# A decode step on one core: attention's softmax and PV by groups of eight heads inside the K/V loop, larger K/V blocks, and a shorter start and end

## The chip, the cores and the metric

One core of one Trainium2 chip runs the whole program. The metric is the device time of one execution in microseconds (us), lower is better. A profiled execution has besides its time a span, from the first to the last recorded instruction; times inside the profile count from the start of the span. "PE" is TensorE's matmuls, "PEld" its weight loads, "DVE" VectorE, "ACT" ScalarE, "POOL" GpSimd and "SPq" the sequencer of SyncE, which issues nearly all transfers here. "PV" is the product of the softmax's weights with V, "PSUM" the memory that TensorE's matmuls write here, and a "ring" is a buffer whose slots are filled in turn and given back when they have been read.

## The reference

One token (x has 1 x 640 elements) goes through attention over a cache and then through a gated feed-forward, all in bf16:

```python
# x (1,1,640); k_cache, v_cache (1,32,4096,128); wq (640,4096); wo (4096,640)
# w_gate, w_up (640,1728); w_down (1728,640)
def _A_ref(x, k_cache, v_cache, wq, wo):
    W = min(4096, max(256, Sk // 4))                 # the last 1024 cached positions
    q = (x @ wq).reshape(B, Sq, 32, 128).transpose(0, 2, 1, 3)
    k, v = k_cache[:, :, Sk - W:, :], v_cache[:, :, Sk - W:, :]
    scores = jnp.einsum("bhqd,bhkd->bhqk", q, k) * (128 ** -0.5)
    o = jnp.einsum("bhqk,bhkd->bhqd", softmax(scores), v)
    return o.transpose(0, 2, 1, 3).reshape(B, Sq, 4096) @ wo

h  = x + _A_ref(layernorm(x), k_cache, v_cache, wq, wo)
h2 = h + (gelu(layernorm(h) @ w_gate) * (layernorm(h) @ w_up)) @ w_down
```

Some 33.9 MB must come in for one token: wq, wo, 1024 positions of K and V for 32 heads, and the three feed-forward weights. There is little arithmetic per byte.

## The kernel before

Everything is loaded by the SP queue in the order wq, K and V by pairs of heads, wo, gate and up, down. K goes through a ring of 8 heads; V stays whole. A head of K arrives as 128 partitions with 8 keys each. TensorE turns its eight 128x128 blocks round (matmuls against an identity), VectorE (even heads) or ScalarE (odd heads) copies the result out of PSUM, and eight one-column matmuls give that head's 1024 scores. Each matmul loads a 128x128 weight first, so it is two instructions of TensorE (the page counts 1316 matmuls and 1316 weight loads).

```python
        def issue_kv(p):                       # p: a pair of heads, 512 KB of K and 512 KB of V
            waits = []
            if p >= KR:                        # KR = 4 pairs in the K ring
                waits.append(ev_tr[2 * (p - KR) + 1])
            s = p % KR
            ev_k[p] = pg.dma("sync", kring[:, 2 * s:2 * s + 2, :], A_k_cache[0, 2 * p:2 * p + 2, S0:SK, :]. ..., st_k, waits=waits)
            ev_v[p] = pg.dma("sync", vbuf[:, 2 * p:2 * p + 2, :], A_v_cache[0, 2 * p:2 * p + 2, S0:SK, :]. ..., st_v)
        ...
        for h in range(NH):                    # the K/V loop
            do_transposes(h)
            if h % 2 == 1:
                p = h // 2 + KR
                if p < NH // 2:
                    issue_kv(p)
            do_evac(h)
            if h - LAG >= 0:
                do_scores(h - LAG)
        for h in range(NH - LAG, NH):
            do_scores(h)
        ev_scdone = ev_sc[NH - 1]
        ...                                    # loads of wo, gate, up, down are issued here
        ev_sts = pg.ins("dve", lambda e: e.tensor_copy(STs[:], psA[:, ST0:ST0 + 256]), waits=[ev_scdone])
        ...                                    # maximum, exp and sums for all 32 heads at once
        for h in range(NH):
            for c in range(8):                 # PV: 256 one-column matmuls
                ... e.matmul(psB[:, col:col + 1], vbuf[:, h, c * DH:(c + 1) * DH], Eb[:, c * 32 + h:c * 32 + h + 1], ...)
        ...
        for g in range(NH // 4):               # output projection: 160 one-column matmuls
            ...
```

x comes in first, with one element per packet, and is the first transfer of the queue. The result leaves through five matmuls and two ScalarE copies:

```python
        xsrc = A_x[0, 0].rearrange("(c p) -> p c", p=128)
        ev_x = pg.dma("sync", xT_b[:], xsrc, st_x, noncontig="tiny x transpose load")
        for k in range(NKC):
            ev_wq.append(pg.dma("sync", wq_v[:, k, :], A_wq[k * 128:(k + 1) * 128, :], st_wq))
        ...
        for c in range(NKC):
            ... e.matmul(dst, outT_b[:, c:c + 1], identb[:, :], start=True, stop=True)
        pg.ins("act", lambda e: e.activation(orow[0:1, 0:256], psD[0:1, 256:512], ACTF.Copy), waits=[ev_fint])
        ev_fin = pg.ins("act", lambda e: e.activation(orow[0:1, 256:D], psE[0:1, 0:384], ACTF.Copy))
```

Of the kernel before, what the change touches and what calls it, by code (L numbers as in the profile page):

```python
# [107 lines left out]
def bass_sequential_preLN__sliding_block_cached__geglu_ffn__decode_kernel(  # L108
# [13 lines left out]
    D = 640  # L122
# [9 lines left out]
    KR = 4  # L132
# [5 lines left out]
    with ExitStack() as es:  # L138
        cnt = [0]

        def S(shape, dt, name=None):
            cnt[0] += 1
            return es.enter_context(nc.sbuf_tensor(name or f"sb{cnt[0]}", list(shape), dt))

        def P(shape, dt, name=None):
            cnt[0] += 1
            return es.enter_context(nc.psum_tensor(name or f"ps{cnt[0]}", list(shape), dt))
# [8 lines left out]
        xT_b = S([128, NKC], BF16, "xT_b")  # L156
        xT = S([128, NKC], FP32, "xT")
        stack1 = S([128, 2 * NKC], FP32, "stack1")
        tot1 = S([128, 2], FP32, "tot1")
        mean1 = S([128, 1], FP32, "mean1")  # L160
        msq1 = S([128, 1], FP32, "msq1")
        var1 = S([128, 1], FP32, "var1")
        lnv1 = S([128, 1], FP32, "lnv1")
        rstd1 = S([128, 1], FP32, "rstd1")
# [6 lines left out]
        kring = S([128, 2 * KR, 1024], BF16, "kring")  # L171
# [6 lines left out]
        STs = S([128, 256], FP32, "STs")  # L178
        m12 = S([128, 2], FP32, "m12")
        m2 = S([128, 1], FP32, "m2")  # L180
        mrow = S([1, NH], FP32, "mrow")
        Dd = S([128, 256], FP32, "Dd")
        Eb = S([128, 256], BF16, "Eb")
# [7 lines left out]
        tot2 = S([128, 2], FP32, "tot2")  # L191
        mean2 = S([128, 1], FP32, "mean2")
        msq2 = S([128, 1], FP32, "msq2")
        var2 = S([128, 1], FP32, "var2")
        lnv2 = S([128, 1], FP32, "lnv2")
        rstd2 = S([128, 1], FP32, "rstd2")
# [19 lines left out]
        orow = S([1, D], BF16, "orow")  # L216
# [7 lines left out]
        QP0, ST0, LN1S, LN2S, GP0 = 0, 160, 416, 426, 436  # L224
        OT0, T10 = 0, 256
        AT0, UP0, FP0, MR0, MX0, RR0 = 0, 160, 230, 300, 428, 460
# [4 lines left out]
        st_k = pg.stream("d_k", 8)  # L231
        st_v = pg.stream("d_v", 8)
        st_wo = pg.stream("d_wo", 8)
# [3 lines left out]
        st_out = pg.stream("d_out", 1)  # L237

# [32 lines left out]
        xsrc = A_x[0, 0].rearrange("(c p) -> p c", p=128)  # L271
        ev_x = pg.dma("sync", xT_b[:], xsrc, st_x, noncontig="tiny x transpose load")
        ev_wq = []
        for k in range(NKC):
            ev_wq.append(pg.dma("sync", wq_v[:, k, :], A_wq[k * 128:(k + 1) * 128, :], st_wq))

        ev = pg.ins("dve", lambda e: e.tensor_copy(xT[:], xT_b[:]), waits=[ev_x])
# [4 lines left out]
            lambda e: e.matmul(psA[:, LN1S:LN1S + 2 * NKC], onesf[:, :], stack1[:, :], start=True, stop=True),  # L282
            waits=[ev_const, ev_stack1],
        )

        def ln_chain(ps_cols, tot, mean, msq, var, lnv, rstd, src_f32, dst_b16, wait_ev):
            ev = pg.ins(
                "dve",
                lambda e: e.tensor_reduce(tot[:], ps_cols.rearrange("p (a b) -> p a b", a=2), axis=AX.X, op=ALU.add),
                waits=[wait_ev],  # L290
            )
            ev = pg.ins("dve", lambda e: e.tensor_scalar(mean[:], tot[:, 0:1], 1.0 / D, None, op0=ALU.mult), waits=[ev])
            ev = pg.ins("dve", lambda e: e.tensor_tensor(msq[:], mean[:], mean[:], ALU.mult), waits=[ev])
            ev_var = pg.ins(
                "dve",
                lambda e: e.scalar_tensor_tensor(var[:], tot[:, 1:2], 1.0 / D, msq[:], op0=ALU.mult, op1=ALU.subtract),  # L296
                waits=[ev],
            )
            ev = pg.ins("act", lambda e: e.activation(lnv[:], var[:], ACTF.Ln, bias=eps_t[:, 0:1], scale=1.0), waits=[ev_var, ev_const])  # L299
            ev_rstd = pg.ins("act", lambda e: e.activation(rstd[:], lnv[:], ACTF.Exp, scale=-0.5), waits=[ev])  # L300
            ev = pg.ins(
                "dve",
                lambda e: e.tensor_scalar(dst_b16, src_f32, mean[:, 0:1], rstd[:, 0:1], op0=ALU.subtract, op1=ALU.mult),  # L303
                waits=[ev_rstd],
            )
            return ev

        ev_xn = ln_chain(psA[:, LN1S:LN1S + 2 * NKC], tot1, mean1, msq1, var1, lnv1, rstd1, xT[:], xn_b[:], ev_ln1mm)

        pg.wait("pe", ev_xn)  # L310
        for k in range(NKC):
            pg.wait("pe", ev_wq[k])
            for h in range(NH):
                pg.ins(
                    "pe",
                    lambda e, k=k, h=h: e.matmul(  # L316
                        psA[:, QP0 + h * NKC + k:QP0 + h * NKC + k + 1],
                        wq_v[:, k, h * DH:(h + 1) * DH],
                        xn_b[:, k:k + 1],
                        start=True,  # L320
                        stop=True,
                    ),
                )
        ev_qdone = pg.cur("pe")
# [9 lines left out]
        ev_k = [None] * (NH // 2)  # L334
        ev_v = [None] * (NH // 2)
        ev_tr = [None] * NH
        ev_evac = [None] * NH
        ev_sc = [None] * NH

        def kslot(h):  # L340
            return (h // 2) % KR * 2 + (h % 2)

        def issue_kv(p):
            waits = []
            if p >= KR:
                waits.append(ev_tr[2 * (p - KR) + 1])
            s = p % KR
            ev_k[p] = pg.dma(
                "sync",
                kring[:, 2 * s:2 * s + 2, :],  # L350
                A_k_cache[0, 2 * p:2 * p + 2, S0:SK, :].rearrange("h (q c) d -> q h (c d)", q=128),
                st_k,
                waits=waits,
            )
            ev_v[p] = pg.dma(
                "sync",
                vbuf[:, 2 * p:2 * p + 2, :],
                A_v_cache[0, 2 * p:2 * p + 2, S0:SK, :].rearrange("h (q c) d -> q h (c d)", q=128),
                st_v,
            )  # L360

        def do_transposes(h):
            waits = [ev_k[h // 2], ev_const]
# [14 lines left out]
        def do_evac(h):  # L378
# [6 lines left out]
            if eng == "dve":  # L385
                ev_evac[h] = pg.ins("dve", lambda e, bank=bank, slot=slot: e.tensor_copy(KT_sb[:, slot, :], psKT[:, bank, :]), waits=waits)  # L386
# [7 lines left out]
        def do_scores(h):  # L394
            waits = [ev_evac[h], ev_qT]
            slot = h % 4
            for c in range(8):
                col = ST0 + c * 32 + h
                ev = pg.ins(
                    "pe",  # L400
                    lambda e, c=c, col=col, slot=slot, h=h: e.matmul(  # L401
                        psA[:, col:col + 1], KT_sb[:, slot, c * 128:(c + 1) * 128], QT_b[:, h:h + 1], start=True, stop=True
# [5 lines left out]
        LAG = 2  # L408
        for p in range(min(KR, NH // 2)):
            issue_kv(p)  # L410
        for h in range(NH):
            do_transposes(h)
            if h % 2 == 1:
                p = h // 2 + KR
                if p < NH // 2:
                    issue_kv(p)
            do_evac(h)
            if h - LAG >= 0:
                do_scores(h - LAG)
        for h in range(NH - LAG, NH):  # L420
            do_scores(h)
        ev_scdone = ev_sc[NH - 1]

        ev_wo = []
        for g in range(NH // 4):
# [3 lines left out]
                    wo_v[:, 4 * g:4 * g + 4, :],  # L429
                    A_wo[g * 512:(g + 1) * 512, :].rearrange("(i p) m -> p i m", p=128),  # L430
# [3 lines left out]
            )  # L434
        ev_wg = []
# [5 lines left out]
        for j in range(6):  # L441
# [11 lines left out]
        ev_sts = pg.ins("dve", lambda e: e.tensor_copy(STs[:], psA[:, ST0:ST0 + 256]), waits=[ev_scdone])  # L453
        pg.ins("pe", lambda e: e.transpose(psB[:, T10:T10 + 128], STs[:, 0:128], identf[:, :]), waits=[ev_sts])  # L454
        ev_t1 = pg.ins("pe", lambda e: e.transpose(psB[:, T10 + 128:T10 + 256], STs[:, 128:256], identf[:, :]))
        ev = pg.ins(
            "dve",
            lambda e: e.tensor_reduce(m12[:], psB[:, T10:T10 + 256].rearrange("p (a b) -> p a b", a=2), axis=AX.X, op=ALU.max),
            waits=[ev_t1],
        )  # L460
        ev_m2 = pg.ins("dve", lambda e: e.tensor_reduce(m2[:], m12[:], axis=AX.X, op=ALU.max), waits=[ev])
        ev_t2 = pg.ins(
            "pe",
            lambda e: e.matmul(psC[0:1, MR0:MR0 + 128], m2[:, 0:1], identf[:, :], start=True, stop=True),  # L464
            waits=[ev_m2],
        )
        ev_mrow = pg.ins(
            "dve",
            lambda e: e.tensor_reduce(
                mrow[:], psC[0:1, MR0:MR0 + 128].rearrange("p (c h) -> p h c", c=4), axis=AX.X, op=ALU.max  # L470
            ),
            waits=[ev_t2],
        )
        ev_maxrep = pg.ins(
            "pe",
            lambda e: e.matmul(psC[:, MX0:MX0 + NH], onesf[0:1, :], mrow[0:1, :], start=True, stop=True),  # L476
            waits=[ev_mrow],
        )
        maxrep_b = psC[:, MX0:MX0 + NH][:, None, :].to_broadcast([128, 8, NH])
        ev_D = pg.ins(  # L480
            "dve",
            lambda e: e.tensor_tensor(
# [187 lines left out]
```

## Time and profile before

| | before |
|---|---|
| time, median of the five runs at hand then | 105.54 us (105.31 to 105.87) |
| span of the profiled execution | 103.3 us |
| moved from memory | 33.90 MB, 328 GB/s over the span |
| TensorE busy | 66.7 us, 1316 matmuls |
| scores of the last head end | 63.8 us |
| down projection starts / ends | 97.25 / 99.81 us |
| last weights have landed | 93.0 us |

### The profile page before, as it was taken

To read this page: it belongs to the slowest core of one execution; us is meant where nothing else is said; L and a number is where in the kernel's file an instruction comes from. 1 tells how busy PE (TensorE), PEld (TensorE's weight loads), DVE (VectorE), ACT (ScalarE), POOL (GpSimd) and SP (SyncE) were. 2 spreads that over 40 slices of the span, in tenths; PEclk is the share of its full clock that TensorE was granted. 3 is DMA by queue.
4 is the path that set the end of the run, shared out by engine and by line. 5 is a ranking of instruction groups with operands and counts; after the bars stand their busy time and mean duration, and the time that the engine had idled before them with its cause. 6 is when DMAs were issued, how large, how long until landed. Compare 5 with 4: busy or idle time off the path is not lost.

```text
span 103.3 us, 2837 instructions
## 1 busy us (share of the span) xinstructions
PE 66.7 (65%) x1316; PEld 62.2 (60%) x1316; DVE 19.8 (19%) x56; ACT 20.2 (20%) x26; POOL 1.5 (1%) x15
## 2 busy tenths in 40 slices
PE   0234430868888888888888885569667592597360
PEld 0134330758887888888888884249666481596350
DVE  0230000222222222222222221340002004102410
ACT  5010000033333333333333333010000000100002
POOL 5000000000000000000000000000000000000000
DMA  0999999999999999999999999999999999930000
GB/s 0 282 412 434 419 438 374 387 387 387 387 384 385 388 386 384 389 384 389 383 385 388 382 369 359 363 363 363 374 412 400 399 397 367 355 125 0 6 0 0
DMA packets 17612, 34.07 MB, mean 330 GB/s; under 512 B 1665, under 2 KB 7490, under 8 KB 16962
## 3 DMA queue, kind: packets, MB, share of 16 engines
q1 hardware_dynamic: 17602, 33.91, 89.0%
q8 instruction: 10, 0.16, 0.7%
HBM read 33.90 MB, written 0.00 MB: 328 GB/s over the span
## 4 chain that ended last, share of the span: by engine, by line
DMA 37%; PE 33%; SPq 14%; DVE 6%; issue 5%; ACT 2%; ACTq 0%
DMA kring<-in_A_k_cache_dram 37%; SPq L79 13%; PE psKT L371 7%; PE psB L507 7%; PE psC L538 5%; PE psA L568 3%; PE psC L568 3%; PE psC L610 2%; PE psA L401 1%; ACT KT_sb L390 1%; PE psC L476 1%; PE psA L554 1%; PE psC L519 1%; PE psC L464 1%; PE psB L454 0%
## 5 line engine op out<-in xcount | busy, mean ns | idle before, releaser
L371 PE MATMUL psKT<-identb,kring 128*128 128x128 bf16 x256 | 32.6, 309 | 7.0 <-DMA kring<-in_A_k_cache_dram 7.0
L371 PEld LDWEIGHTS psKT<-identb,kring 128*128 128x128 bf16 x256 | 24.7, 140 | 8.4 <-DMA kring<-in_A_k_cache_dram 8.4
L390 ACT ACTIVATE KT_sb<-psKT 128x1024 bf16<-128x1024 bf16 x16 | 16.4, 1023 | 40.6 <-PE psA L401 25.5
L386 DVE COPY KT_sb<-psKT 128x1024 bf16<-128x1024 bf16 x16 | 11.1, 692 | 30.8 <-PE psA L401 30.2
L401 PEld LDWEIGHTS psA<-QT_b,KT_sb 128*128 128x128 bf16 x256 | 13.0, 115 | 0.8 <-ACT KT_sb L390 0.8
L401 PE MATMUL psA<-QT_b,KT_sb 128*128 128x1 bf16 x256 | 12.5, 171 | 0.7 <-ACT KT_sb L390 0.7
L316 PE MATMUL psA<-xn_b,wbig 128*128 128x1 bf16 x160 | 5.0, 166 | 9.2 <-DMA wbig<-in_A_wq_dram 9.2
L316 PEld LDWEIGHTS psA<-xn_b,wbig 128*128 128x128 bf16 x160 | 4.7, 104 | 9.6 <-DMA wbig<-in_A_wq_dram 7.5
L507 PE MATMUL psB<-Eb,vbuf 128*128 128x1 bf16 x256 | 7.6, 165 | 1.8 <-issue 1.8
L507 PEld LDWEIGHTS psB<-Eb,vbuf 128*128 128x128 bf16 x256 | 7.5, 104 | 2.1 <-issue 2.1
L538 PE MATMUL psC<-OT_b,wbig 128*128 128x1 bf16 x160 | 4.6, 165 | 2.0 <-issue 1.2
L538 PEld LDWEIGHTS psC<-OT_b,wbig 128*128 128x128 bf16 x160 | 4.4, 104 | 2.2 <-issue 1.3
L299 ACT ACTIVATE lnv<-var,eps_t 128x1 f32<-128x1 f32 x2 | 0.6, 295 | 23.3 <-DVE var L296 23.3
L568 PE MATMUL psA<-hn_b,wg_sb 128*128 128x1 bf16 x70 | 3.2, 170 | 1.7 <-DVE hn_b L303 1.7
L568 PEld LDWEIGHTS psA<-hn_b,wg_sb 128*128 128x128 bf16 x70 | 2.8, 107 | 2.0 <-DVE hn_b L303 1.8
L610 PE MATMUL psC<-act_b,wd_sb 128*128 128x1 bf16 (+1 forms) x70 | 2.1, 165 | 2.4 <-DVE act_b L600 2.4
L610 PEld LDWEIGHTS psC<-act_b,wd_sb 128*128 128x128 bf16 (+1 forms) x70 | 2.0, 104 | 2.5 <-DVE act_b L600 2.4
L282 PE MATMUL psA<-stack,onesf 128*128 128x10 f32 x2 | 0.6, 362 | 4.4 <-DVE stack L279 4.4
L568 PE MATMUL psC<-hn_b,wu_sb 128*128 128x1 bf16 x70 | 3.2, 170 | 0.0
L282 PEld LDWEIGHTS psA<-stack,onesf 128*128 128x128 f32 x2 | 0.5, 310 | 4.4 <-issue 4.4
L568 PEld LDWEIGHTS psC<-hn_b,wu_sb 128*128 128x128 bf16 x70 | 2.8, 107 | 0.1
L327 DVE TENSOR_REDUCE QT_f<-psA 128x32 f32<-128x160 f32 x1 | 0.3, 325 | 12.8 <-PE psA L316 12.8
(75 smaller groups left out, 21.4 us busy)
## 6 DMA issues: line engine op xcount, KB each, us to landing
kring<-in_A_k_cache_dram SPq DMA_DIRECT2D x16, 512.0 KB, 8.6
vbuf<-in_A_v_cache_dram SPq DMA_DIRECT2D x16, 512.0 KB, 9.6
wbig<-in_A_wq_dram SPq DMA_DIRECT2D x5, 1024.0 KB, 9.5
wbig<-in_A_wo_dram SPq DMA_DIRECT2D x8, 640.0 KB, 10.7
wg_sb<-in_B_w_gate_dram SPq DMA_DIRECT2D x5, 432.0 KB, 10.6
wu_sb<-in_B_w_up_dram SPq DMA_DIRECT2D x5, 432.0 KB, 11.2
wd_sb<-in_B_w_down_dram SPq DMA_DIRECT2D x6, 320.0 KB, 11.2
wd_sb<-in_B_w_down_dram SPq DMA_DIRECT2D x1, 160.0 KB, 8.2
```

What stands on the lines that cost most here:

```text
L79: e.dma_start(out_ap, in_ap, **kw).then_inc(sem, 16)
L282: lambda e: e.matmul(psA[:, LN1S:LN1S + 2 * NKC], onesf[:, :], stack1[:, :], start=True, stop=True),
L316: lambda e, k=k, h=h: e.matmul(psA[:, QP0 + h * NKC + k:QP0 + h * NKC + k + 1], wq_v[:, k, h * DH:(h + 1) * DH], xn_b[:, k:k + 1], start=True,
L371: lambda e, c=c, bank=bank, s=s: e.transpose(psKT[:, bank, c * 128:(c + 1) * 128], kring[:, s, c * DH:(c + 1) * DH], identb[:, :]),
L386: ev_evac[h] = pg.ins("dve", lambda e, bank=bank, slot=slot: e.tensor_copy(KT_sb[:, slot, :], psKT[:, bank, :]), waits=waits)
L390: lambda e, bank=bank, slot=slot: e.activation(KT_sb[:, slot, :], psKT[:, bank, :], ACTF.Copy),
L401: lambda e, c=c, col=col, slot=slot, h=h: e.matmul(psA[:, col:col + 1], KT_sb[:, slot, c * 128:(c + 1) * 128], QT_b[:, h:h + 1], start=Tru ...
L464: lambda e: e.matmul(psC[0:1, MR0:MR0 + 128], m2[:, 0:1], identf[:, :], start=True, stop=True),
L507: lambda e, h=h, c=c, col=col: e.matmul(psB[:, col:col + 1], vbuf[:, h, c * DH:(c + 1) * DH], Eb[:, c * 32 + h:c * 32 + h + 1], start=True ...
L538: lambda e, h=h, m=m, col=col: e.matmul(psC[:, col:col + 1], wo_v[:, h, m * 128:(m + 1) * 128], OT_b[:, h:h + 1], start=True, stop=True),
L568: lambda e, k=k, m=m, msz=msz, col=col, wsb=wsb, ps=ps: e.matmul(ps[0:msz, col:col + 1], wsb[:, k, m * 128:m * 128 + msz], hn_b[:, k:k + 1 ...
L610: lambda e, k=k, m=m, ksz=ksz, col=col: e.matmul(psC[:, col:col + 1], wd_sb[0:ksz, k, m * 128:(m + 1) * 128], act_b[0:ksz, k:k + 1], start ...
```

## The change

Its intent is to take softmax and PV of the first three groups of eight heads out of the serial tail and lay them beside the K/V transfers; 60 of the output projection's 160 matmuls fill waits in the softmax of the last group. K and V come by blocks of four heads (1 MB each), the K ring holds 12 heads, and a group's steps are put on an agenda, to be emitted during later iterations of the loop. Besides, wo comes in four transfers instead of eight, and there are 260 dummy matmuls between the Q projection's chunks, meant to bring TensorE's clock up, a one-step shorter layer norm and GELU, x as five rows on ScalarE's queue with a small transpose, and a last step of one matmul and one copy.

The diff, cut to its core (renamed tiles and PSUM columns are left out):

```diff
-    KR = 4
+    HB = 4
+    NB = NH // HB
+    KR = 3
+    GH = 8
+    NG = NH // GH
...
+        ev_x = pg.dma("act", x5[:, :], A_x[0, 0].rearrange("(c p) -> c p", p=128), st_x)
-        xsrc = A_x[0, 0].rearrange("(c p) -> p c", p=128)
-        ev_x = pg.dma("sync", xT_b[:], xsrc, st_x, noncontig="tiny x transpose load")
...
+            for d in range(80 if k == 3 else 45):
+                pg.ins(
+                    "pe",
+                    lambda e: e.matmul(psD[:, 511:512], identb[:, :], identb[:, 0:1], start=True, stop=True),
+                )
...
-                kring[:, 2 * s:2 * s + 2, :],
-                A_k_cache[0, 2 * p:2 * p + 2, S0:SK, :].rearrange("h (q c) d -> q h (c d)", q=128),
+                kring[:, HB * s:HB * s + HB, :],
+                A_k_cache[0, HB * b:HB * b + HB, S0:SK, :].rearrange("h (q c) d -> q h (c d)", q=128),
...
+        def schedule_group(g, it0):
+            at(it0, lambda: g_step_stscopy(g))
+            at(it0 + 1, lambda: g_step_t1(g))
+            at(it0 + 2, lambda: g_step_row(g))
+            at(it0 + 3, lambda: g_step_mx(g))
+            at(it0 + 4, lambda: g_step_sums(g))
+            at(it0 + 4, lambda: g_step_pv(g, 0, 4))
+            at(it0 + 5, lambda: g_step_pv(g, 1, 4))
+            at(it0 + 6, lambda: g_step_rrep(g))
+            at(it0 + 6, lambda: g_step_pv(g, 2, 4))
+            at(it0 + 7, lambda: g_step_pv(g, 3, 4))
+            at(it0 + 8, lambda: g_step_ot(g))
...
-        for h in range(NH - LAG, NH):
-            do_scores(h)
+        for hs in range(NH - LAG, NH):
+            do_scores(hs)
+            if hs % GH == GH - 1:
+                schedule_group(hs // GH, it)
+            run_agenda(it)
+            it += 1
+        at(it, lambda: at_part(0, 0, 2))       # output projection of heads 0 to 3, and so on
+        at(it + 1, lambda: at_part(0, 1, 2))
+        at(it + 2, lambda: at_part(1, 0, 2))
...
-        for c in range(NKC):                   # five matmuls and two ScalarE copies
-            ...
+            lambda e: e.matmul(psD[0:NKC, FIN0:FIN0 + 128], outT_b[:, 0:NKC], identb[:, :], start=True, stop=True),
+        ev_fin = pg.ins("dve", lambda e: e.tensor_copy(orow5[:, :], psD[0:NKC, FIN0:FIN0 + 128]), waits=[ev_fint])
```

## The prediction

> **What bounds the kernel now.** I read the page's 40 slices first, then the stretches, the chain of waits in order of time, and the DMA issues. Numbers are microseconds (us) of the profile's span, 103.3; the measured median, 105.54, is 2.24 more, and I add that at the end.
>
> The slices (tenths of busy time in 2.6 us each):
>
> ```profile
> PE   0234430868888888888888885569667592597360
> DMA  0999999999999999999999999999999999930000
> ```
>
> The transfers are full from 2.6 to 90 us; nothing but TensorE and small work fills the last five slices. The stretches say the same with rates (columns: stretch, length, busy us and count of PE, PEld, DVE, ACT, POOL; clock; DMA share; GB/s):
>
> ```profile
> 28.00:60.00 32.00, 27.20 (x383) 26.21 (x381) 8.30 (x12) 11.82 (x13) 0.00 (x0) 1.00 1.05 386
> 75.00:90.00 15.00, 8.86 (x266) 8.42 (x265) 2.20 (x10) 0.50 (x2) 0.00 (x0) 1.00 1.04 390
> 90.00:103.30 13.30, 7.70 (x193) 6.98 (x189) 2.17 (x13) 0.96 (x3) 0.00 (x0) 1.00 0.11 36
> ```
>
> In the K/V stage one pair of heads takes 2.72 us, which is 1.05 MB at 386 GB/s, and TensorE has a small rest before each pair (start, length, work, idle time before it):
>
> ```profile
> 24.99 1.03 PE L371 MATMUL psKT<-identb,kring 128*128 128x128 bf16 x8 [0.43 <-DMA kring<-in_A_k_cache_dram]
> 25.82 0.40 PE L401 MATMUL psA<-QT_b,KT_sb 128*128 128x1 bf16 x8
> 26.08 1.01 PE L371 MATMUL psKT<-identb,kring 128*128 128x128 bf16 x8
> 26.89 0.40 PE L401 MATMUL psA<-QT_b,KT_sb 128*128 128x1 bf16 x8
> 27.70 1.04 PE L371 MATMUL psKT<-identb,kring 128*128 128x128 bf16 x8 [0.41 <-DMA kring<-in_A_k_cache_dram]
> ```
>
> So that stage is bound by the transfers with 0.4 of 2.7 us to spare on TensorE. Afterwards the chain changes hands (start, length, what):
>
> ```profile
> 63.37 0.44 PE psA L401 x8
> 63.83 0.43 DVE STs L453
> ...
> 68.63 5.39 PE psB L507 x181
> 74.02 1.80 issue
> 75.82 2.14 PE psB L507 x75
> ...
> 79.25 1.52 PE psC L538 x51
> 80.77 1.24 issue
> 82.01 3.89 PE psC L538 x109
> ...
> 97.25 2.56 PE psC L610 x70
> 99.83 0.24 DVE ffn L617
> ```
>
> From 63.8 on, softmax, PV, output projection, second norm, gate/up, GELU and down projection run in series, 39.5 us, while the weights for them land behind their backs. The last weights come here (KB each, us from issue to landing):
>
> ```profile
> wd_sb<-in_B_w_down_dram SPq DMA_DIRECT2D x1, 80.0 KB, 7.9
> ```
>
> The timeline of the issuing queue puts that last issue at 85.06, so it lands at 93.0. The down projection starts at 97.25, 4.3 us later. **Hence the bound: transfers to 63, TensorE's serial tail afterwards, and only about 10.3 us of the end come after the last landing.**
>
> [...] eight transposes of 314 ns each end within 1.03 us, (1.03-0.314)/7 = 0.102 apart. The page's clock of 1.00 is no evidence; the spacing is. [...] a block of 32 one-column matmuls in 0.99 us is (0.99-0.165)/31 = 27 ns apart, but 109 of them take 3.89 in the chain, 36 ns each, so I price long runs at 34 to 36 and short ones at 27. [...] the two "issue" rests, 1.80 and 1.24 us, lie 128 matmuls (256 instructions with their weight loads) apart, and the packed DMA records have 16 KB instruction packets at 73.4 and 79.6, 1.1 us each, just before TensorE resumes. [...]
>
> **The change part by part.**
>
> *Softmax and PV by groups of 8 heads inside the K/V loop.* Per group TensorE had 8 x 1.07 = 8.6 us of transposes and scores. It gains 64 PV matmuls, 64 x 0.027 = 1.7, and a small chain (transpose, row, maximum, sums, reciprocal), of which the old one's matmuls took 0.23 to 0.65 each; smaller ones, about 1.4 together. Sum 11.7 against 10.8 of transfers for the group: TensorE becomes the slower of the two by 8%, but the first 10 heads carry no such work, and K is now buffered for 12 heads instead of 8. DVE and ACT have room (8.3 and 11.8 of 32 us).
>
> *Dummy matmuls.* 45, 45, 45, 80, 45 behind the five wq chunks: 260 more, each with an increment. Chunks land 2.5 us apart; 77 matmuls at 0.034 take 2.6, the 112 take 3.8. That alone moves the first transposes from 19.55 to about 21.2. They also eat instructions: [...] I get rests of 1.8 and 1.6 us and the first transposes near 24. I choose 24.
>
> *Loop end.* 10 heads x 1.07 from 24 gives 34.7; 22 more at 1.07 = 23.5, three groups' extra work 9.4, the last evacuation and scores 1.0: 68.6, against 63.8. The K reissues (after 4, 8, 12, 16, 20 heads) come some 4 us before the queue runs dry, so transfers should not pause.
>
> *Tail.* After 68.6 only group 3 is left: its chain about 3.6 (old 4.4, with narrower tiles), with 60 projection matmuls hidden inside; PV 64 x 0.034 = 2.2; then 100 projection matmuls, 3.4; reduction 0.3. Sum 9.5, plus about 1 for one instruction rest: 79.1 against 85.9 + 0.3. Norm: old 3.1 to the first gate matmul less one DVE step 0.2, so 82.0. Gate/up 5.9 (the last wu landed at 73.0 + 13.7 = 86.7 by its issue and its longest landing, 0.8 earlier now, and its matmuls run last, after 87): 87.9. GELU 2.5 less one step 0.2: 90.2. Down projection 2.6: 92.8.
>
> *Start and end.* x goes to ACT's queue in five rows, so wq is issued 0.5 earlier, and 640 two-byte packets vanish (about 5 us over 16 engines, 0.3): the last landing moves from 93.0 to 92.2. Then five last matmuls and the reduction can start at 92.7. One final matmul and one DVE copy instead of five matmuls and two ACT copies: the 3.5 us from the old reduction to the end lose about 0.9, leaving 2.6.
>
> Sum: the later of TensorE's 92.8 and the landing's 92.7, then 2.6: span 95.4, and with 2.24 **97.7 us, 7.4% less**. Both limits meet within their errors.
>
> **The rivals.** *A: the weights' landing alone is the end.* If the dummies cost less than I charge, or the loop is quicker, TensorE waits for the last panel: 92.7 + 2.6 + 2.2 = 97.5, no better. For it: transfers already run at 1.04 to 1.07 share and no byte is removed; against it: 24.
>
> *B: TensorE gets late.* Each us added to the start, loop or tail comes through once it passes the landing. Two or three more instruction rests of 1.5, which dense one-column runs invite, make 99.5 to 101. For it: the two rests of the old tail[...].
>
> *C: the K ring starves the queue.* If transposes of block b finish after the queue is drained, every us of gap moves the landing. It needs TensorE 4 us later than I think; result 99 to 102.
>
> *D: the dummies warm the clock.* Transposes below 107 ns would bring the loop back to the transfers' pace, and the result falls to A, 97.5, not lower. Against it: 256 PV matmuls in a row were followed by gate/up no faster.
>
> **Range and chances.** A and D are a floor near 97.5, less if the stream starts and flows a little better (96.7). B and C stretch upwards, so the range is lopsided: 96.7 to 100.5. To miss 2% (103.4) both B and C would have to hit hard: faster 0.95, same 0.04, slower 0.01.
>
> **What would show it.** Right: last wd landing at 92 to 93 with DMA still full to 90; transposes starting near 24, 106 ns apart; no idle before them "<-DMA kring" after the first heads; scores ending near 68.6; gate/up starting near 82; down projection either running straight or waiting for wd. Wrong: gaps in the DMA slices (C); many "issue" rests of over 1 us (B); transposes 60 to 80 ns apart (D); the first transposes at 20 to 21 (my instruction count for the dummies fails, TensorE early, but the end unchanged); a last landing far from 92.2, which would move the result by the same amount.

The sum came to 92.8 us for TensorE and 92.7 for the landing, to 92.8 + 2.6 = 95.4 of span, and with 2.24 to 97.7. The rests of 1.8 and 1.6 us among the dummies, which put the first transposes near 24 instead of 21.2, were the author's estimate; without them TensorE would end near 90.0 and the landing alone, 92.7 + 2.6 + 2.24, gives 97.5. The 0.5 us by which wq is issued earlier is the time that SPq takes to issue the x load in the trace of the kernel before, 0.46 us.

The same trace has these numbers: most transposes start 106 or 107 ns after the one before (194 of 255 steps); the 640 two-byte packets of x took 5.02 us, all added up; in PV and in gate/up alike the median step between one-column matmuls is 27 ns, which is the "no faster" under rival D. The page's clock of 1.00 is no evidence because that trace holds no clock record at all.

## More of the kernel before

The page of the kernel before gives the busy time by engine, and among the transfer queues one for instructions (packets, MB, share of the 16 transfer engines' time):

```profile
PE 66.7 (65%) x1316; PEld 62.2 (60%) x1316; DVE 19.8 (19%) x56; ACT 20.2 (20%) x26; POOL 1.5 (1%) x15
...
q8 instruction: 10, 0.16, 0.7%
```

No compute engine is busy over two thirds of the time, and the 16 transfer engines, which the page has at 89.0%, stand idle in the last four slices, so no total tells what bounds the kernel; it has to be read stage by stage. The ten instruction packets of 16 KB each look like nothing at 0.7% of the transfer engines' time.

## The result, and the profile after

Ratios here are the mean time of one kernel's fast runs over that of the other's of the same rounds, so they are not quite the ratio of the medians quoted beside them.

| | before | after |
|---|---|---|
| median of all runs | 105.49 us (105.23 to 105.87, 15 runs) | 97.58 us (97.21 to 97.7, 8 runs) |
| ratio, 95% interval | | 0.9252 (0.9238 to 0.9266) |
| profiled execution: time / span | 105.59 / 103.3 us | 97.7 / 95.9 us |
| scores of the last head end | 63.8 us | 67.6 us |
| gate/up starts | 89.0 us | 81.5 us |
| down projection starts | 97.25 us | 89.67 us |
| last weights have landed | 93.0 us | 92.8 us |

The slices of the page after, and its instruction queue. Each digit is a 40th of the span, 2.4 us:

```profile
PE   0269828639997909999999999999699822994551
...
PEclk9999999999999999555555555555555555555555
DMA  2999999999999999999999999999999999999500
...
q8 instruction: 12, 0.20, 0.8%
```

TensorE is now full where it used to be at 8 tenths, and the slices without transfers at the end are two instead of four. The clock row is to be read with care: it has 9 for the first 38 us, but the packed clock record begins only at 28.05 us, and the 24 transposes at 22.80 below take 2.72 us, (2.72 - 0.31) / 23 = 0.105 apart, the same pace as later under the row's 5 (mostly 106 or 107 ns from 38.29 on). The K/V stage after (columns as in the prediction):

```profile
20.00:61.00 41.00, 37.21 (x670) 35.89 (x669) 14.24 (x36) 14.78 (x16) 0.00 (x0) 0.72 1.05 385
```

The transfers run at the same 385 GB/s in the K/V stage as before (386). So the change has not made the stream faster; it has filled TensorE beside it, and what is left between the last landing and the end of the span has gone from 10.3 us to 3.1.

TensorE's timeline after shows where it stood still (start, length, work, idle time before it and what ended that):

```profile
14.65 0.46 PE L341 MATMUL psD<-identb 128*128 128x1 bf16 x12 [2.12 <-issue]
...
20.84 0.89 PE L330 MATMUL psA<-xn_b,wbig 128*128 128x1 bf16 x28 [2.57 <-issue]
...
22.80 2.72 PE L404 MATMUL psKT<-identb,kring 128*128 128x128 bf16 x24
...
36.00 0.62 PE L404 MATMUL psKT<-identb,kring 128*128 128x128 bf16 x8 [2.23 <-DMA kring<-in_A_k_cache_dram]
...
38.37 1.01 PE L404 MATMUL psKT<-identb,kring 128*128 128x128 bf16 x8
...
78.10 0.40 PE L648 MATMUL psA<-OT_b,wbig 128*128 128x1 bf16 x9 [1.21 <-issue]
...
91.50 0.43 PE L758 MATMUL psC<-act_b,wd_sb 128*128 128x1 bf16 x10 [0.60 <-DMA wd_sb<-in_B_w_down_dram]
92.25 0.90 PE L758 MATMUL psC<-act_b,wd_sb 128*128 128x1 bf16 x20 [0.32 <-DMA wd_sb<-in_B_w_down_dram]
```

Three things are to be seen. Two rests of "issue" lie at the start, one among the dummies and one within the Q projection (before 20.84), and a third in the output projection: TensorE waits for nothing that the profile shows. Each time a 16 KB instruction packet has just gone through (it began at 12.07, 18.34 and 75.60, and TensorE resumed 2.50 to 2.58 us later), so I read them as waits for instructions. At 36.00 a head takes 0.62 us and TensorE had waited 2.23 us for K, while at 38.37 a head takes 1.01. And the down projection, which is last, twice waits for its own weights. The chain of waits says that this is what sets the end:

```profile
83.17 9.03 DMA wd_sb<-in_B_w_down_dram
...
92.25 0.95 PE psC L758 x20
...
93.71 0.28 PE psD L772
...
94.01 0.28 DVE orow L775
```

Before, no transfer was in the chain after 60.2 us. Now the last transfers of weights are in it, and from the end of the last matmul (93.20) to the end of the span it is 2.7 us, where before it was 3.5.

### The profile page after: what moved, and what is told of

Read it like the earlier page. It is cut to its first block, busy times and chain, and to the rows that moved or that the text cites. A ratio compares the mean times of both kernels' runs of the same rounds, so it can differ in the third digit from the quotient of the medians.

```text
span 95.9 us, 3397 instructions
## 1 busy us (share of the span) xinstructions
PE 72.5 (76%) x1596; PEld 68.7 (72%) x1596; DVE 23.2 (24%) x80; ACT 20.0 (21%) x27; POOL 1.5 (2%) x15
## 4 chain that ended last, share of the span: by engine, by line
SPq 37%; DMA 28%; PE 25%; issue 6%; DVE 1%
SPq L79 37%; PE psKT L404 10%; DMA kring<-in_A_k_cache_dram 10%; DMA wd_sb<-in_B_w_down_dram 9%; DMA wbig<-in_A_wq_dram 9%; PE psD L341 5%; PE psA L330 3%; PE psE L551 2%; PE psB L440 1%; PE psC L758 1%; PE psA L440 1%; PE psC L567 1%; PE psC L498 0%; PE psD L772 0%; DVE orow L775 0%
## 5 line engine op out<-in xcount | busy, mean ns | idle before, releaser
L341 PE MATMUL psD<-identb 128*128 128x1 bf16 x260 | 7.8, 165 | 2.1 <-issue 2.1
L341 PEld LDWEIGHTS psD<-identb 128*128 128x128 bf16 x260 | 7.4, 104 | 2.2 <-issue 2.2
L551 PE MATMUL psE<-Eb,vbuf 128*128 128x1 bf16 x256 | 8.9, 165 | 0.0
L551 PEld LDWEIGHTS psE<-Eb,vbuf 128*128 128x128 bf16 x256 | 7.9, 104 | 0.3
L648 PE MATMUL psA<-OT_b,wbig 128*128 128x1 bf16 x160 | 5.2, 166 | 1.6 <-issue 1.2
L648 PEld LDWEIGHTS psA<-OT_b,wbig 128*128 128x128 bf16 x160 | 4.9, 105 | 2.1 <-issue 1.5
L440 PE MATMUL psA<-QT_b,KT_sb 128*128 128x1 bf16 x128 | 6.1, 169 | 0.0
L440 PEld LDWEIGHTS psA<-QT_b,KT_sb 128*128 128x128 bf16 x128 | 6.1, 110 | 0.0
L440 PE MATMUL psB<-QT_b,KT_sb 128*128 128x1 bf16 x128 | 6.1, 168 | 0.0
L440 PEld LDWEIGHTS psB<-QT_b,KT_sb 128*128 128x128 bf16 x128 | 6.0, 109 | 0.0
```

Source lines behind the costliest of these rows:

```text
L341: lambda e: e.matmul(psD[:, 511:512], identb[:, :], identb[:, 0:1], start=True, stop=True),
L440: lambda e, c=c, col=col, slot=slot, h=h, ps=ps: e.matmul(ps[:, col:col + 1], KT_sb[:, slot, c * 128:(c + 1) * 128], QT_b[:, h:h + 1], sta ...
L551: lambda e, h=h, c=c, col=col: e.matmul(psE[:, col:col + 1], vbuf[:, h, c * DH:(c + 1) * DH], Eb[:, h * 8 + c:h * 8 + c + 1], start=True, ...
L648: lambda e, h=h, m=m, col=col: e.matmul(psA[:, col:col + 1], wo_v[:, h, m * 128:(m + 1) * 128], OT_b[:, h:h + 1], start=True, stop=True),
```

## The experiments

All ran on the same inputs; "before" in the same rounds had medians between 105.45 and 105.57 us. Times are medians with the lowest and highest run, ratios are to the kernel before. Unless said otherwise a kernel is the changed one with one edit (e5, e6, e10 and e12 have no dummies besides), and its output agreed with the reference. That agreement is weak evidence for attention here: with these inputs attention's part of the output is so small that three kernels which are wrong (e6, e9, e10) passed as well.

### e1: without the dummy matmuls

```diff
-            for d in range(80 if k == 3 else 45):
+            for d in range(0):
```

> The changed kernel without its 260 dummy matmuls. Theory A (the landing of the last weights is the end, and each 16 KB instruction packet holds up one of the 16 transfer engines by 1.1 us): two packets fewer, the slowest engine trails the first by 2 us at the last weights as in the kernel before, instead of 3.5, the last landing moves from 92.8 to about 91.5 and the time to 96.3. The clock never warms (transposes 107 ns apart all through), first transposes near 19.6 instead of 22.8. Rival B (the end does not depend on the instruction packets): last landing 92.6 to 92.8, time 97.3 to 97.6. Rival C (the warm clock from the dummies is worth something): slower than the changed kernel, 98.3 or more.

Measured: 97.50 us (97.36 to 97.6), 0.9238 (0.9223 to 0.9254). The transposes started at 19.74 instead of 22.80, the scores ended 1.2 us sooner (66.42), and the end did not move. Its chain has the same last link:

```profile
82.30 9.77 DMA wd_sb<-in_B_w_down_dram
```

Theory A's number, 96.3, was missed: nine packets were left before the last landing, not eight, and its spread stayed at 3.36 us (below). So 260 dummies neither help nor harm: the 3 us that they cost at the start are taken up by waits for K and for weights later. The clock rose without them too: the trace's clock record has full speed from 23.0 to 26.4 and from 60.6 to 67.4.

### e2: the kernel before with the new x load and the new end only

```diff
 (to the kernel before)
+        ev_x = pg.dma("act", x5[:, :], A_x[0, 0].rearrange("(c p) -> c p", p=128), st_x)
-        ev_x = pg.dma("sync", xT_b[:], xsrc, st_x, ...)
+        (one matmul, one VectorE copy and five rows out instead of five, two and one)
```

> The kernel before with only the new x load and the new final transpose and copy; softmax, PV and projection stay after the loop. Theory A (most of the gain comes from moving softmax, PV and projection into the loop): end shorter by 0.9, start sooner by 0.5 to 1.2, so 103.4 to 104.1, and 5.8 or more are left for the grouping. Rival (the start and end are the bulk): 101 or less.

Measured: 103.26 us (103.14 to 103.4), 0.9785 (0.9769 to 0.9802). Start and end are worth (1 - 0.9785) x 105.57 = 2.3 us of the 7.9. The other 5.6 belong to the rest: groups, blocks and ring, dummies, and the shorter norm and GELU.

### e3: the changed kernel with the old end

> The changed kernel with the old end: five matmuls into one row, two ACT copies. It lies behind the last landing, so theory A has it in full: 0.9 slower, 98.5. Rival (the output transfer with five rows costs as much as it saves): within 0.3 of the changed kernel.

The edit is the last hunk of the diff taken back. Measured: 98.47 us (98.31 to 98.5), 0.9332 (0.9316 to 0.9347), so 0.9 us more. Its chain of waits after the reduction:

```profile
93.45 0.37 PE psD L778 x2
93.82 0.33 PE psE L778 x3
...
94.17 0.37 ACT orow L781
```

These links and 0.37 us more of ScalarE's sequencer stand where the changed kernel has 0.28 and 0.28 us.

### e4: the changed kernel with the old x load

```diff
-        ev_x = pg.dma("act", x5[:, :], A_x[0, 0].rearrange("(c p) -> c p", p=128), st_x)
+        xsrc = A_x[0, 0].rearrange("(c p) -> p c", p=128)
+        ev_x = pg.dma("sync", xT_b[:], xsrc, st_x, noncontig="tiny x transpose load")
```

> The changed kernel with the old x load: 640 two-byte packets on the weights' queue before wq. The first wq chunk landed 1.27 us sooner in the changed kernel, K blocks too. Theory A (the stream is full, so what it starts later it ends later): last landing 1.2 later, 98.8. Rival (the last landing is set by the slowest transfer engine, which moved only 0.2 between the two kernels, not by the start): 0.0 to 0.4 slower.

Measured: 99.26 us (98.98 to 99.63), 0.9408 (0.9375 to 0.9441), 1.7 us more; the last landing was 94.0, 1.2 us later. The 640 two-byte packets ahead of wq (5.02 us of packet time in the trace before) cost more than I had estimated (0.8 with the issue).

### e5: down's weights with fewer, longer rows

```diff
-            for d in range(80 if k == 3 else 45):
+            for d in range(0):
...
-                B_w_down[j * 256:(j + 1) * 256, :].rearrange("(i p) m -> p i m", p=128),
+        wd_rows = B_w_down[0:1664, :].rearrange("(p j) m -> p j m", j=KC_FF - 1)   # four transfers
...
-    wsb[:, k, m * 128:m * 128 + msz]
+    wsb[:, k, m:m + 128 * (KC_FF - 1):KC_FF - 1] if m < KC_FF - 1 else wsb[:, k, F - msz:F]
```

> The changed kernel without dummies, and with the FFN's hidden units dealt to partitions as f = 13 p + m, so that w_down's rows come in packets of 3840 to 5120 bytes instead of 1280 (gate/up take every 13th column as weights). Theory A (the landing of the last weights is the end): 2.1 MB at about 395 instead of 342 GB/s, the rates of the 3456 and 1280 byte packets in the trace of before, is 0.8 us less, so 96.7. Rival (packets are not the limit, or the strided weight loads slow gate/up): 97.5[...].

Cut from the rival is a figure for slow weight loads, which no trace had shown. The two rates are those of the trace before: its 3456 byte packets took 139.8 ns on average and its 1280 byte ones 59.9, which over 16 engines is 396 and 342 GB/s.

Measured: 99.03 us (98.51 to 100.45; the slowest is the profiled one), 0.937 (0.9328 to 0.9412); the fast runs are 98.51 to 99.35. This kernel has no dummies, so it is to be held against e1 (97.50). In the only trace, of the slow run, the last landing came at 92.1, against 92.7 in e1. But for gate and up the weight columns now lie 13 apart, and this is slower on TensorE. A block of 14 of them in the timeline of e5:

```profile
80.94 1.08 PE L711 MATMUL psB<-hn_b,wg_sb 128*128 128x1 bf16 x14 [1.54 <-DVE hn_b L304]
```

The next block starts at 81.95, 1.01 us later, where the changed kernel's blocks follow each other in 0.58 (82.10 after 81.52). In the same trace the down projection's 70 matmuls, whose columns lie side by side, take 2.11 us, 0.028 apart, and these are 0.07 apart. Ten blocks made the down projection start at 93.4 instead of 89.7, and TensorE set the end. The sooner landing could not be cashed in; the version fails.

### What the packed records show of the last landing

The page counts 16 transfer engines, and the trace records 16 increments of a semaphore for each of these transfers, one by one. I read each increment as one engine that has ended its part; the trace does not name the engine. So it can be seen which transfer has a straggler. In the kernel before, the first and last increment of a transfer lie 0.7 us apart up to 13.6 us. Then an instruction packet (16 KB, 1.0 to 1.1 us long) goes through at 15.6 us, and from there one increment is over 1.3 us behind the first. After each further packet (28.7, 39.5, 50.4, 61.3, 73.4, 79.6, 85.7) the number of such late ones goes up by one, until there are eight, with the spread still at 2.0 to 2.1. In the changed kernel the packets come sooner, since it has more instructions, and with the ninth at 69.3 the spread jumps from 1.92 to 3.23: one increment is now over 2.6 us late, and later up to four. The transfers behind it stay that way to the end. The same jump, by 1.2 to 1.5 us, comes with the ninth packet wherever the stream has no gap: in e1 at 82.4 (2.05 to 3.52), in e3 at 69.6, in e4 at 68.5, in e5 at 82.5 and in e6 at 87.7 (1.89 to 3.07). This suggests that the packets go round eight engines, and the ninth delays one that is already late. The same reading of the last weights' transfer in every kernel that ran:

```text
kernel                    instruction packets   first      last       spread
                          begun before it       increment  increment
before                     8                    90.85      92.97      2.12
e2 (start and end only)    8                    90.04      91.92      1.88
e11 (below)                8                    89.83      91.93      2.10
e9 (below)                 8                    89.51      91.26      1.75
e12 (below)                8                    89.43      91.38      1.94
e1 (no dummies)            9                    89.32      92.68      3.36
e6 (below)                 9                    89.58      92.39      2.82
e5 (slow run)              9                    88.98      92.08      3.10
after                     11                    89.23      92.79      3.56
e3 (old end)              11                    89.28      92.52      3.24
e4 (old x)                12                    90.50      94.02      3.53
e7 (below)                13                    92.26      95.33      3.07
e8 (below)                12                    95.89      98.21      2.32
e10 (below)               11                   124.67     127.03      2.35
```

The time of the kernel waits for the last increment. In the changed kernel the first one came 1.6 us sooner than before, and the last only 0.2. (e8 and e10 are the exceptions with their smaller spreads. Their streams have gaps, and after one the late increments are gone: none is late at 49.8 us in e8 and at 97.1 in e10. In e7 the pause at 31 to 34 us takes the late ones from four to none but the one of a new packet, and the jump, from 1.83 to 3.35, comes only with the packet at 91.8, the thirteenth in all and the ninth since the pause. So in these runs what counts is the packets since the last gap.)

### e6: fewer TensorE instructions

```diff
-            for h in range(NH):
+            for h in range(NH if k == NKC - 1 else 0):      # Q: 32 matmuls instead of 160, no dummies
-                        psA[:, QP0 + h * NKC + k:QP0 + h * NKC + k + 1],
+                        psA[:, QP0 + h * NKC:QP0 + h * NKC + NKC],
```

> Wrong result on purpose: the changed kernel without dummies and with 32 Q matmuls instead of 160, all wq chunks still awaited, so that TensorE's stream is one 16 KB block shorter and nothing else moves. In the traces each instruction packet adds one late transfer engine, and the ninth makes one late twice: the trailing engine's delay goes from 2.0 to 3.5 us. Theory A (that ninth packet sets the last landing): the ninth packet comes after 88, the trail stays at 2.0, the last landing near 91.3 instead of 92.7, the time 96.0. Rival (the trail comes from elsewhere, such as the smaller packets of the last weights): 97.3 to 97.6.

Measured: 97.52 us (97.28 to 97.78), 0.9244 (0.922 to 0.9268). There were still nine packets, the ninth at 87.7 us, just ahead of the last transfers, and the last landing was at 92.39. So it did not test the theory as meant: a kernel with eight was needed.

### e9: eight instruction packets

```diff
 (to e6)
-                for c in range(8):
+                for c in range(0, 8, 2):                    # PV: 128 matmuls instead of 256
-                            psE[:, col:col + 1],
+                            psE[:, col:col + 2],
```

> Wrong result on purpose: as the run with fewer Q matmuls, and each PV matmul takes two columns of weights for two output columns, so 128 matmuls fewer again: in the run before this one the ninth instruction packet still came at 87.7, now there should be at most eight before the last landing. Theory A (the ninth packet sets the last landing): the trailing engine stays at 1.9 us to the end, the last landing near 91.4 instead of 92.4, time 96.4 to 96.6. Rival (the trail or the landing comes from elsewhere): 97.3 to 97.6.

Measured: 96.13 us (96.08 to 96.28), 0.9117 (0.9103 to 0.9131). The page counts eight instruction packets, and the landing that its chain waits for is 1.2 us sooner than after (82.23 + 8.81 against 83.17 + 9.03):

```profile
q8 instruction: 8, 0.13, 0.6%
```

```profile
82.23 8.81 DMA wd_sb<-in_B_w_down_dram
```

The spread of the last transfer is 1.75 us. The same bytes are moved, and the first increment is even 0.28 us later than in the changed kernel; only the stragglers are gone. Against e6 the difference is one packet, and 128 matmuls that lie on neither chain after 47 us.

### e7: 128 dummies more

```diff
-            for d in range(80 if k == 3 else 45):
+            for d in range(108 if k == 3 else 70):
```

> The changed kernel with 128 dummies more, one 16 KB block. First transposes 5 to 6 us later, near 28.5; the 2.9 us that TensorE waited for K at 30 and 34 are used up, so the scores end 3 us later, near 70.6, and the down projection, which needed no longer than 92.2 by TensorE alone, ends near 95.2, past the last landing. Theory A (two limits that nearly meet): 99.0 to 100.5. Rival (transfers hide TensorE by a wide margin): within 0.5 of 97.6.

Measured: 100.45 us (99.61 to 101.76; one run slow), 0.9494 (0.9446 to 0.9543); the fast runs are 99.61 to 100.66. The size is about as expected, the way is not the one of TensorE's tail. The rates by slice of its page, each 2.46 us:

```profile
GB/s 47 403 416 426 423 413 392 386 389 389 382 386 247 88 404 392 389 387 386 386 385 388 389 378 382 365 362 361 363 359 379 409 409 417 403 381 360 232 12 1
```

The stream pauses around 31 to 34 us (247 and 88 GB/s). The transposes started at 28.58, so the first ring slots were given back late: the next K block was issued at 32.40, 1.3 us after the last transfer in flight had begun to end (31.09). The pause goes into every later landing; the first increment of the last transfer is 3.0 us later than after. This is the prediction's rival C. It shows as well how much slack the changed kernel has: in it the same block is issued at 26.61, 4.7 us before the last transfer ahead of it begins to end (31.35).

### e8: a K ring of 8 heads

```diff
-    KR = 3
+    KR = 2
```

> The changed kernel with K buffered for 8 heads instead of 12. Block 2 of K can only be asked for when block 0 is transposed, at 26.6, and by then the queue holds nothing: V1 lands from 25.9 on. Theory A (the larger ring pays for the late start of TensorE): a gap of 2 to 2.5 us in the transfers, seen as a step in the landings after 26 us and kept to the end, 99.6 to 100.2. Rival (8 heads are enough as in the kernel before): within 0.4 of 97.6.

Measured: 100.85 us (100.31 to 103.12; the profiled run was slow), 0.9542 (0.949 to 0.9594); the fast runs are 100.31 to 101.33. The transfers paused between 20 and 45 us, where they moved 339 GB/s against 385 (from the slow run). With dummies ahead and blocks of four heads, 8 heads of K are too few.

### e11: start, end and blocks, but no groups

```diff
 (to e2)
-    KR = 4
+    HB = 4
+    KR = 3          # K and V by 1 MB blocks, ring of 12 heads; softmax and PV stay after the loop
```

> The kernel before with the new x load and the new end, and now also K and V in 1 MB blocks of four heads with a ring of 12 heads, but softmax, PV and projection still after the loop. Theory A (the blocks and the ring are worth nothing by themselves, only moving the work into the loop is): 103.0 to 103.5 as with the small transfers. Rival (larger transfers quicken the stream): 102 or less.

Measured: 103.84 us (103.2 to 104.08), 0.9836 (0.9802 to 0.987), against 103.26 for e2. Larger blocks and a longer ring bring nothing by themselves. So of the 7.9 us, 2.3 are start and end, and the rest comes with the groups, for which the ring gives the slack (e8). The one-step shorter norm and GELU were not tried alone; they are within that rest.

### e10: K and V with packets of 4 KB

```diff
-            for d in range(80 if k == 3 else 45):
+            for d in range(0):
...
-                A_k_cache[0, HB * b:HB * b + HB, S0:SK, :].rearrange("h (q c) d -> q h (c d)", q=128),
+                src[0, HB * b + x:HB * b + HB:2, S0:SK, :].rearrange("h (q c) d -> q h (c d)", q=64),   # x = 0, 1
```

> Wrong result on purpose, to price the transfers: the changed kernel without dummies, K and V in packets of 4 KB (two heads on 64 partitions each, two transfers per block, the same bytes) instead of 2 KB; all else works on the wrongly laid out data. Theory A (the landing is the end and the packet's size sets the rate: 3456 byte packets moved 6% more per time than 2048 byte ones): K and V take 40.9 instead of 43.4, last landing 90.3, then TensorE's own limit near 91.4 takes over, time 96.0. Rival (half of the partitions per transfer loses what the packets gain): 97.5 or slower.

Measured: 131.83 us (131.21 to 132.45), 1.2496 (1.2441 to 1.255). Each transfer now fills 64 partitions with packets twice as long. The stretch of the K/V stage in it:

```profile
20.00:85.00 65.00, 37.02 (x564) 35.77 (x565) 12.94 (x31) 13.81 (x15) 0.00 (x0) 1.00 1.04 216
```

At the same share of busy transfer engines (1.04) only 216 GB/s were moved instead of 385. The theory that led to it has fallen: whatever longer packets may give (in the trace before, 3456 byte packets moved 396 GB/s over 16 engines and 2048 byte ones, 88.0 ns each, 372), the arrangement as a whole costs far more. Packet size and half the partitions were not separated.

### e12: VectorE takes the scores of 12 heads

If eight packets are worth 1.3 us, a correct kernel should get there too. Here VectorE computes the scores of heads 1, 3 and 5 of each group (12 of 32) from K as it lies, a multiplication with q repeated over the partitions and a sum (0.61 and 1.22 us for a head in its chain of waits, 1.83 together). That saves TensorE 16 matmuls for each of them, and the dummies are gone too.

```diff
-            for d in range(80 if k == 3 else 45):
+            for d in range(0):
...
+        def do_offload(h):
+                lambda e, j=j, s=s, b=b: e.tensor_tensor(
+                    kq[:, b, :]. ..., kring[:, s, :]. ..., qrow[:, j, :][:, None, :].to_broadcast([128, 8, DH]), ALU.mult),
+                lambda e, b=b, col=col: e.tensor_reduce(
+                    STs[:, col:col + 8], kq[:, b, :].rearrange("p (c d) -> p c d", d=DH), axis=AX.X, op=ALU.add),
...
         for h in range(NH):
-            do_transposes(h)
+            if h % GH in OFF:              # OFF = (1, 3, 5)
+                do_offload(h)
+            else:
+                do_transposes(h)
```

> A version with right results that has TensorE's stream shorter: the changed kernel without dummies, in which VectorE computes the scores of 12 of the 32 heads (K times the head's q, spread over the partitions by three matmuls, then a sum over 128), so that 192 transposes and score matmuls, 378 instructions with their loads and less the three new ones, are gone from TensorE. Theory A (the last landing is the end, and the ninth instruction packet sets it): at most eight instruction packets before the last landing, trail 1.7 to 2.0 us, last landing 91.3, time 96.1 to 96.4. Rival (VectorE, about 1.8 us per head here, holds up the K ring or TensorE): a gap in the transfers or a softmax chain that waits for VectorE, 97.5 or more.

Measured, five runs: 96.25 us (96.06 to 96.39), 0.9125 (0.9101 to 0.9149). It beats both kernels. Its page and its chain:

```profile
PE 56.9 (60%) x1146; PEld 51.9 (55%) x1147; DVE 38.1 (40%) x95; ACT 21.6 (23%) x30; POOL 1.6 (2%) x16
...
q8 instruction: 9, 0.15, 0.7%
```

```profile
83.82 7.56 DMA wd_sb<-in_B_w_down_dram
```

The ninth packet comes at 90.7, after the last transfer has begun to land, so eight count. The last landing is 91.38 and its spread 1.94, as the table has it. TensorE has 450 matmuls fewer than in the changed kernel, 15.6 us of busy time, and the gain over it is 1.3 us, what the sooner landing gives: the end still hangs on the stream. Because the comparison on the chip hardly sees attention, this kernel was also compared with the reference in a simulation with weights and caches scaled up. Repeated with wq, wo and the caches 20 times as large, it gave relative errors under 0.01 for this kernel and for the changed one, and over 1 for e9, which is wrong.

## Why the prediction was right

The time was 97.58 us against 97.7 predicted, and the direction, the main mechanism and the size were right. By its steps:

- *The tail's work fits beside the stream.* Right. e11 shows that blocks and ring alone bring nothing, so the groups bring what start and end (2.3 us, e2) do not. The scores were predicted to end at 68.6 and did at 67.6; gate/up at 82.0, measured 81.5; down at 90.2, measured 89.67.
- *Dummies and instruction rests.* The rests at the start were 2.12 and 2.57 us instead of 1.8 and 1.6, the first transposes at 22.80 instead of 24. e1 shows that all of this leaves the end where it is.
- *A third rest.* Of the rests that rival B feared in the tail there was one, 1.21 us, as the sum had allowed (about 1).
- *K waits.* That the transposes would have no idle time for K before them after the first heads was wrong: there were waits of 0.68 and 2.23 us. TensorE was ahead of the stream, since it began 1.2 us sooner than predicted and by the next point; no run separates the two.
- *Clock.* The prediction counted on transposes 106 ns apart throughout. Rival D was half right: from 28.05 to 38.29 the clock record has full speed, and the transposes in it are 55 to 56 ns apart, with scores among them, but TensorE then only waited for K. It brought nothing, as rival D had it ("97.5, not lower"). The clock rose 7.2 us after the last rest, which ended at 20.84. It fell back at 38.29, with no rest since longer than the 2.23 us before 36.00, and then the record stays at 0.5 though TensorE was over 90% busy from 36 to 67 us. That the dummies raised it is not shown, since it rose in e1 too.
- *Start.* Undersized: 0.8 us was predicted for the landing, e4 shows 1.2, and e2's last landing is 1.05 sooner than before.
- *Last landing.* 92.2 was predicted, 92.8 measured. The step "the last landing moves from 93.0 to 92.2" has the gain of the start in it and misses a loss: the fast transfer engines ended 1.6 us sooner, but the slowest trailed by 3.56 instead of 2.12 us. The prediction used the instruction packets for TensorE's rests alone and did not ask what they do to the engines that carry them. e9 and e12, with eight packets, land at 91.3 and 91.4.
- *End.* One matmul and one copy: 0.9 predicted, 0.9 in e3.
- *Pace of matmuls.* The prediction prices one-column matmuls at 27 ns in short runs and 34 to 36 in long ones. In both traces most of them start 26 or 27 ns after the one before (823 of 993 steps before, 1059 of 1226 after). The 36 ns come from 3.89 us in the chain for 109 of them, a piece that lasts until the reduction starts; the timeline has the 109 in 3.06 us. What sets the pace no run shows.
- *Span to time.* 2.24 was added (95.4 + 2.24 is 97.64, put down as 97.7); in the profiled execution it was 97.7 - 95.9 = 1.8. The span was predicted 0.5 us too short and this term 0.4 too long. The closeness of the sum is partly luck.
- *Rivals.* A describes the end best: TensorE waits for the last panels (0.60 and 0.32 us), and the down projection would have ended at about 89.67 + 2.6 = 92.3 without waits, against 93.2. Both limits did meet within an error of 1 us. C did not come, but e7 and e8 make it come, at 2.6 and 3.1 us (fast runs alone).

That instruction packets delay the last landing is shown as far as this: the count of late increments rises with them in the traces, the spread jumps with the ninth since the last gap in all seven kernels that have one before the end (e7 included), and two different edits that get down to eight gain 1.45 and 1.3 us. No run changed the number of packets and nothing else. Which rule sends a packet to which transfer engine stays open, and so does the reason why the clock rose where it did.

## What to carry to other kernels

When a serial tail follows a saturated stream, moving its work beside the stream gains until the stream's last landing is the end; from then on less work for TensorE alone is worth nothing (e1: 97.50 us against 97.58), and the stream counts: its start, its gaps, its stragglers. More work can still cost (e5: 99.03 us). Read not only when a transfer has landed but how far its sixteen increments lie apart, and count the instruction packets, since a kernel of many small matmuls brings many of them (here 9 packets with 1146 matmuls in e12, 10 with 1316 before, 12 with 1596 after), and here they went with the stragglers. Before adding work ahead of a ring's consumer, work out how long the queue can go on without a slot being given back: here transposes 3 us later cost nothing (e1 against the changed kernel), and another 5.8 us cost 2.6 (e7).
